# The last block's order by row halves, its stores on two queues, and one tile of batch 4 placed 1.2 slots later

## The chip, the core and the metric

The kernel runs on one core of one Trainium2 chip. The metric is the device time of that core in microseconds (us), as the median of repeated executions. One further execution was taken with the hardware profiler; all rows shown below are from that one.

The core's engines appear in the profile as PE (TensorE matmul), PEld (TensorE weight load), DVE (VectorE), ACT (ScalarE), POOL (GpSimd) and SP (SyncE, which here only issues DMAs). SPq and ACTq are the DMA issues on the queues of SP and ACT.

## What is computed

For each of 8 batches and 8 heads, with 576 positions and a head size of 64:

```python
kv  = einsum('bhsd,bhse->bhde', k, v)
out = einsum('bhsd,bhde->bhse', q, kv)
out = out / sqrt(mean(out*out, -1) + 1e-6) * g_norm      # -> x, 512 columns per position
xn  = (x - mean(x)) / sqrt(var(x) + 1e-6) * g_ln
y   = x + relu(xn @ w_ch1) @ w_ch2                       # 512 -> 2048 -> 512
```

## The kernel before

**Blocks.** The 8 x 576 rows are worked on as nine blocks of 512 rows, four tiles of 128 rows each: one block for the first 512 rows of each batch, and a last block, "rem", that gathers the 64 remaining rows of all eight batches. A block has two stages on PE: `mm1` (line 684; 512 to 2048, ReLU on ACT) and the second product (2048 to 512). The tiles of block b+1 are prepared while block b is on PE: matmul `o_ps` (line 302), square on ACT (`sq`, line 308), sum on DVE (`ss`, line 379), root on ACT (`rms`, line 387), then on DVE the reciprocal (`inv`, line 394), two scalings (lines 383 and 401), the negated mean (line 405) and the centred copy `xc` (line 426), and a DMA transpose from SP (line 437) that gives `xT_blk`. The variance (`dev`, line 419) is an ACT instruction of its own.

**The second product in seven products.** From block 1 on, the second product is a two-by-two block product made of seven half-sized products instead of eight. Its row sums S1, S2, S4, S3 are DVE additions (lines 515 to 518, `row_sums`), made in three pieces; the last piece is placed at the first four ticks of the second stage. Blocks 1 to 7 go through `mm2_seven` (line 547). Block 3 uses the order p1, p4, p6, p5, p2, p3, p7. Of these, p6 multiplies S2 into `p_y`, DVE then reads `p_y` into `u2` (line 566), and p3 adds S3's product to the same bank, so p3 cannot start before that reading.

**The order of work.** Instructions are emitted in program order to each engine, and each engine takes its own in that order. PE's loops call `tick()` (line 778), and an agenda written out by hand puts everything else at a slot, which `at` (line 769) turns into a tick: a block has 16 ticks for `mm1` and, from block 1 on, 14 for the seven products, so slots past 16 of a block shrink by 14/16. Within a tick the agenda's entries are sorted by slot, and the row sums have -1, which puts them first. `plan_tile` (line 455) places a tile's first part (`o_ps`, `sq`, `ss`) at a slot, its second part (root to `xc`) two slots later, its transpose at 4.5 slots later, and its variance at a slot of its own. `keep_q` (line 234), a POOL copy of the batch's remaining q rows, is placed half a slot after the last tile's first part.

The lines that place batch 4's tiles are 965 to 972. They are reached while block 3 is on PE.

**The last block.** `mm2_seven_last` (line 621) takes the two tiles of each half one after the other instead of together. For tile t it does p_x, p_q, p_y, p_z and the second part of p_y, after which DVE writes the two halves of a lower-row tile (`o(1, 0)`, `o(1, 1)`, line 651), which `put(1)` stores; then the second part of p_x and p_l, after which DVE writes an upper-row tile, which `put(0)` stores. Tile 0 is finished wholly before tile 1 starts. `store` (line 731) makes two DMAs of 64 partitions for the last block, one always on SP, the other on the queue given as `upper`. Tile 1's last product and its last store are cut in two column halves.

Of the kernel before, what the change touches and what calls it, by code (L numbers as in the profile page):

```python
# [14 lines left out]
def kernel(  # L15
# [11 lines left out]
    nc = tc.nc  # L27
    f32 = mybir.dt.float32
    bf16 = mybir.dt.bfloat16
    AF = mybir.ActivationFunctionType  # L30
    ALU = mybir.AluOpType
# [26 lines left out]
    ps_m = ctx.enter_context(tc.psum_pool(name="ps_m", bufs=1))  # L58
    ps_out = ctx.enter_context(tc.psum_pool(name="ps_out", bufs=2))
    ps1 = ctx.enter_context(tc.psum_pool(name="ps1", bufs=3))  # L60
    ps2 = ctx.enter_context(tc.psum_pool(name="ps2", bufs=2))
# [172 lines left out]
    def keep_q(b):  # L234

        nc.gpsimd.tensor_copy(qj[:, b], qts.pop(b)[:, J, :, :64])
# [203 lines left out]
    def main_tile(b, j, pool=None, tag="ops"):  # L440
        q_t, kvp = qts[b], held[b]
        if b not in blks:
            blks[b] = new_block()
        return Tile([(slice(0, 128), lambda hp: q_t[:, j, hp, :], kvp)], blks[b], j, pool, tag)
# [41 lines left out]
    H2, C2 = nDe // 2, Dm // 2  # L486
# [5 lines left out]
    def m1_q(b, rows, odd):  # L492
        return m1s[b][:, odd::2, rows * 256:rows * 256 + 256]

    def w2_q(odd, cols):
        return w2_sb[:, odd::2, cols * C2:cols * C2 + C2]
# [24 lines left out]
    def product(dst, a, w, start, stop, ts=(0, 1), c0=0, c1=256):  # L521


        for t in ts:
            tick()
            for i in range(H2):
                nc.tensor.matmul(dst[:, t - ts[0], :c1 - c0], lhsT=a[:, i, t * 128:(t + 1) * 128],  # L527
                                 rhs=w[:, i, c0:c1], start=start and t == ts[0] and i == 0,
                                 stop=stop and t == ts[-1] and i == H2 - 1,
                                 skip_group_check=True)  # L530

    def outs(b):
        x_blk = blks[b][0]
        o_sb = [outp.tile([128, 2, Dm], f32, tag="osb", name="o_sb") for _ in range(2)]

        def x(rows, cols):
            return x_blk[:, 2 * rows:2 * rows + 2, cols * C2:cols * C2 + C2]

        def o(rows, cols):
            return o_sb[rows][:, :, cols * C2:cols * C2 + C2]  # L540

        return x, o, o_sb

    def half(pool, tag, name):
        return pool.tile([128, 2, C2], f32, tag=tag, name=name)
# [75 lines left out]
    def mm2_seven_last(b):  # L621
        V, G = nc.vector, nc.gpsimd
        S1, S2, S3, S4 = sums.pop(b)
        a11, a12, a22 = m1_q(b, 0, 0), m1_q(b, 0, 1), m1_q(b, 1, 1)
        b11, b21, b22 = w2_q(0, 0), w2_q(1, 0), w2_q(1, 1)
        x_all, _, o_sb = outs(b)
        v0_t, v1_t, qv_t, w22_t, u2_t = (half(fpool, n, n) for n in ("v0", "v1", "u3", "r5", "u2"))
        banks = (((ps1, "p1"), (ps1, "p1"), (ps2, "p2"), (ps2, "p2"), (ps_m, "misc")),
                 ((ps1, "p1"), (ps1, "p1"), (ps_out, "ops"), (ps_out, "ops"), (ps1, "p1"),
                  (ps2, "p2")))  # L630
        for t in range(2):
            def x(rows, cols):
                return x_all(rows, cols)[:, t]

            def o(rows, cols):
                return o_sb[rows][:, t, cols * C2:cols * C2 + C2]

            def part(dst, a, w, start, stop, c0=0, c1=C2):
                product(dst, a, w, start, stop, (t,), c0, c1)

            def put(rows, c0=0, c1=Dm, upper=nc.scalar):
                store(b, 2 * rows + t, o_sb[rows][:, t:t + 1], c0, c1, upper)

            ends = ((0, C2),) if t == 0 else ((0, C2 // 2), (C2 // 2, C2))
            p_x, p_q, p_y, p_z, *p_l = (pool.tile([128, 1, C2], f32, tag=tag, name="p_s")
                                        for pool, tag in banks[t])
            v0, v1, qv, w22, u2 = (a[:, t] for a in (v0_t, v1_t, qv_t, w22_t, u2_t))
            r0, r1 = (rstds[b][:, 2 * rows + t:2 * rows + t + 1] for rows in range(2))

            def scaled_add(dst, src, r, other):  # L650
                V.scalar_tensor_tensor(dst, in0=src, scalar=r, in1=other,
                                       op0=ALU.mult, op1=ALU.add)

            part(p_x, a11, b11, True, False)
            nc.scalar.activation(v1, p_x[:, 0], func=AF.Copy, scale=r1)
            nc.scalar.activation(v0, p_x[:, 0], func=AF.Copy, scale=r0)
            G.tensor_add(w22, v1, x(1, 1))
            part(p_q, a22, T4, True, True)
            scaled_add(qv, p_q[:, 0], r1, v1)
            G.tensor_add(qv, qv, x(1, 0))  # L660
            part(p_y, S2, T2, True, False)
            scaled_add(u2, p_y[:, 0], r0, v0)
            G.tensor_add(u2, u2, x(0, 1))
            part(p_z, S1, T1, True, True)
            scaled_add(w22, p_z[:, 0], r1, w22)
            scaled_add(u2, p_z[:, 0], r0, u2)
            part(p_y, S3, T3, False, True)
            scaled_add(o(1, 0), p_y[:, 0], r1, qv)
            scaled_add(o(1, 1), p_y[:, 0], r1, w22)
            put(1)  # L670
            part(p_x, a12, b21, False, True)
            scaled_add(o(0, 0), p_x[:, 0], r0, x(0, 0))
            if t:
                put(0, 0, C2)
            for p, (c0, c1) in zip(p_l, ends):
                part(p, S4, b22, True, True, c0, c1)
                scaled_add(o(0, 1)[:, c0:c1], p[:, 0, :c1 - c0], r0, u2[:, c0:c1])
            if t:
                put(0, C2)
            else:  # L680
                put(0, upper=nc.sync)
            del p, p_l, p_x, p_q, p_y, p_z

    def mm1(b, t0, n, c0=0, c1=nDe):
        blk, m1 = blks[b], m1_of(b)
# [45 lines left out]
    def store(b, ts, o_sb, c0=0, c1=Dm, upper=None):  # L731

        n = o_sb.shape[1]
        if b == "rem":
            dst = out[:, :S_LO, :].rearrange("(t f) (p j) e -> f j p t e", j=JJ, f=2)[:, J]
            for half, engine in enumerate((nc.sync, upper)):
                engine.dma_start(dst[half, :, ts:ts + n, c0:c1],
                                 o_sb[half * 64:half * 64 + 64, :, c0:c1])
            return
        eng = nc.gpsimd if b == 0 or b == 1 and ts >= 2 else nc.sync  # L740
        for half in range(2):
            src = o_sb[half * 64:half * 64 + 64, :, c0:c1]
            if b == 0:
                j = 2 * ts + half
                dst = (out[b, :S_LO, :].rearrange("(p j) e -> p j e", j=JJ)[:, j:j + 1] if ts < 2
                       else out[b, S_LO:, :].rearrange("(p j) e -> p j e", j=J)[:, j - J:j - J + 1])
            else:
                dst = (out[b, S_LO:, :].rearrange("(p j) e -> p j e", j=J) if half else
                       out[b, :S_LO, :].rearrange("(p j) e -> p j e", j=JJ))[:, ts:ts + n]
            eng.dma_start(dst[:, :, c0:c1], src)  # L750
# [18 lines left out]
    def at(slot, fn):  # L769

        i, r = divmod(slot, 32)
        blocks = [*range(B), "rem"]
        if r > 16 and i < len(blocks) and blocks[int(i)] in SEVEN:
            r = 16 + (r - 16) * 14 / 16
        s = sum(30 if x in SEVEN else 32 for x in blocks[:int(i)]) + r
        agenda.setdefault(int(s + 1e-6), []).append((s, fn))

    def tick():
        for _, fn in sorted(agenda.pop(clock[0], []), key=lambda e: e[0]):
# [17 lines left out]
    t = [main_tile(0, 0)] + [main_tile(0, i, *((ps1, "p1"), (ps_m, "misc"), (ps2, "p2"))[i - 1])  # L797
                             for i in range(1, 4)]
# [163 lines left out]
    at(268, lambda: rstd_of("rem"))  # L962


    for b, at_q, at_o in ((3, 52, (68.5, 72.5, 76.5, 83)), (4, 81, (96.5, 102.7, 109, 115)),
                          *((b, 32 * b - (46.4 if b == 5 else 47.2), tuple(32 * b - i for i in (34.5, 27.3, 20.1, 12.9)))
                            for b in range(5, B))):
        at(at_q, lambda b=b: turn_q_dma(b))
        for j, o in enumerate(at_o):
            plan_tile(o, lambda b=b, j=j: main_tile(b, j), o + 4.5, False, 32 * b - 13.4 + 3.5 * j)  # L970
        at(at_o[-1] + .5, lambda b=b: keep_q(b))
        at(32 * b + 6, lambda b=b: rstd_of(b))
# [15 lines left out]
    for ts in range(4):  # L988
        p2 = p2s[ts]
# [46 lines left out]
```

## Time and profile before

| | |
|---|---|
| median of 3 runs (lowest to highest) | 278.20 us (278.18 to 278.21) |
| the profiled execution's own time | 278.19 us |
| its span in the trace | 276.0 us |
| PE busy | 268.8 us (97%) |
| DVE, ACT, POOL busy | 197.7, 185.5, 116.6 us |
| block 3's stretch on PE, 107.39 to 135.92 us | 28.53 us |
| the last block's seven products start at | 259.53 us |

The profile's span is the time in the trace from the core's first to its last instruction; the execution's time is 2.2 us longer. In the rows, "start us, us" are an instruction's start from the span's start and its length; a merged row covers several instructions of one kind (x8). "[0.18 <-DVE u L566]" says that the engine was idle for 0.18 us just before, and what released it. Instructions of one engine are pipelined, so that the next may start before the last has ended. Matmul ends are modelled.

### The profile page before, as it was taken

Reading aid. Unit: us, or ns where it says so; the run is one execution under the profiler, and the core shown is the slowest. Engines: PE = TensorE matmul, PEld = TensorE weight load, DVE = VectorE, ACT = ScalarE, POOL = GpSimd, SP = SyncE. Lnnn points to the kernel's source line nnn. Section 1 sums busy time; section 2 is a strip of 40 time slices with the busy share of each in tenths; the row PEclk is TensorE's granted clock in tenths of the full one; section 3 lists DMA queues with packets and bytes.
Section 4 is the critical chain, followed back from the end, with each engine's and each line's share of the span. In section 5 each row is a group of like instructions: output and inputs, shape, how many; then the busy total and the mean of one; then the engine's idle time right before and its main releaser. Section 6 shows DMA issues by size and latency. Waiting matters only on the chain.

```text
span 276.0 us, 6784 instructions
## 1 busy us (share of the span) xinstructions
PE 268.8 (97%) x2674; PEld 194.8 (71%) x2674; DVE 197.7 (72%) x464; ACT 185.5 (67%) x414; POOL 116.6 (42%) x143
## 2 busy tenths in 40 slices
PE   8899999999999999999999999999999999999993
PEld 3589855999889986468745874587458745874683
DVE  6676437897996895999679856985797379823564
ACT  3567755898759685768576857786877487746610
POOL 8842440991099007901870196017101800280140
PEclk9999999999999999999999999999999999999999
DMA  7999999979979993996299829960711161005032
GB/s 215 199 207 205 197 194 192 202 179 194 113 123 158 184 187 83 151 221 125 31 190 252 116 34 189 246 118 19 171 21 20 21 171 21 20 19 154 1 76 78
DMA packets 63880, 36.57 MB, mean 132 GB/s; under 512 B 34016, under 2 KB 60900, under 8 KB 63848
## 3 DMA queue, kind: packets, MB, share of 16 engines
q0 software_dynamic: 29104, 19.34, 47.9%
q1 hardware_dynamic: 34152, 15.81, 27.8%
q10 hardware_dynamic: 592, 0.98, 1.0%
q8 instruction: 21, 0.34, 0.5%
q14 instruction: 11, 0.09, 0.1%
HBM read 36.71 MB, written 9.44 MB: 167 GB/s over the span
## 4 chain that ended last, share of the span: by engine, by line
PE 84%; DVE 7%; DMA 4%; ACT 2%; issue 1%; POOL 1%; DVEq 0%; POOLq 0%
PE p L694 41%; PE p_y L527 8%; PE p_z L527 8%; PE p_x L527 8%; PE p L716 5%; PE p_s L527 4%; DMA w_sb<-in_moe_w_ch_dram 4%; PE p_q L527 4%; PE o_ps L302 2%; PE kv_ps L275 2%; DVE ss L379 1%; DVE S L517 1%; ACT m L697 1%; DVE o_ps L383 1%; DVE x_blk L401 1%
## 5 line engine op out<-in xcount | busy, mean ns | idle before, releaser
L694 PE MATMUL p<-xT_blk,w_sb 128*128 128x128 bf16 (+2 forms) x1024 | 131.7, 286 | 0.6 <-DMA w_sb<-in_moe_w_ch_dram 0.3
L694 PEld LDWEIGHTS <-w_sb 128*128 128x128 bf16 x1024 | 78.7, 98 | 44.9 <-issue 0.7
L697 ACT ACTIVATE m<-p 128x512 bf16<-128x512 f32 x144 | 85.5, 598 | 35.2 <-PE p L694 33.0
L527 PEld LDWEIGHTS <-m 128*128 128x128 bf16 x512 | 49.4, 98 | 7.7 <-issue 0.6
L379 DVE TENSOR_REDUCE ss<-sq 128x8 f32<-128x512 f32 x35 | 23.8, 680 | 24.6 <-ACT sq L308 24.4
L527 PEld LDWEIGHTS <-S 128*128 128x128 bf16 x392 | 37.5, 98 | 4.5 <-DVE S L516 0.3
L582 POOL TENSOR_TENSOR q<-q,x_blk 128x512 f32<-128x512 f32 x5 | 6.4, 1290 | 69.7 <-ACT q L561 69.7
L527 PE MATMUL p_x<-w_sb,m 128*128 128x256 bf16 x224 | 27.3, 273 | 0.0
L419 ACT ACTIVATE dev<-x_blk,st_blk 128x512 f32<-128x512 f32 x36 | 26.0, 722 | 0.3 <-DVE st_blk L405 0.2
L609 POOL TENSOR_TENSOR u<-u,x_blk 128x512 f32<-128x512 f32 x7 | 8.9, 1268 | 39.5 <-DVE u L566 39.5
L383 DVE TENSOR_TENSOR o_ps<-o_ps,inv 128x512 f32<-128x512 f32 x33 | 23.1, 700 | 3.1
L401 DVE SCALAR_TENSOR_TENSOR x_blk<-o_ps,g_norm_sb 128x512 f32<-128x512 f32 x33 | 22.8, 691 | 1.1
L308 ACT ACTIVATE sq<-o_ps 128x512 f32<-128x512 f32 x35 | 21.0, 599 | 3.6 <-PE o_ps L302 3.6
L515 DVE TENSOR_TENSOR S<-m 128x768 bf16<-128x768 bf16 (+2 forms) x22 | 12.7, 582 | 12.2 <-ACT m L697 12.2
L426 DVE TENSOR_SCALAR xc<-x_blk,st_blk 128x512 bf16<-128x512 f32 x32 | 18.6, 581 | 1.1
L387 ACT ACTIVATE rms<-ss,eps_sb 128x8 f32<-128x8 f32 x36 | 10.8, 299 | 11.7 <-DVE ss L379 11.3
L566 DVE SCALAR_TENSOR_TENSOR u<-p_y,rstd,v 128x256 f32<-128x256 f32 x28 | 12.2, 476 | 5.3 <-PE p_y L527 5.3
L716 PE MATMUL p<-w_sb,m 128*128 128x512 bf16 x64 | 15.0, 379 | 0.0
L561 ACT ACTIVATE v<-p_x,rstd 128x256 f32<-128x256 f32 x28 | 11.0, 478 | 5.3 <-PE p_x L527 5.3
L527 PE MATMUL p_y<-T,m 128*128 128x256 bf16 x112 | 13.9, 272 | 0.2 <-DVE u L566 0.2
L527 PE MATMUL p_z<-w_sb,S 128*128 128x256 bf16 x112 | 13.5, 273 | 0.0
L527 PE MATMUL p_y<-T,S 128*128 128x256 bf16 x112 | 13.5, 273 | 0.0
(149 smaller groups left out, 367.6 us busy)
## 6 DMA issues: line engine op xcount, KB each, us to landing
out_dram<-o_sb SPq DMA_DIRECT2D x26, 256.0 KB, 4.5
w_sb<-in_moe_w_ch_dram POOLq DMA_DIRECT2D x6, 512.0 KB, 13.7
q_in<-in_q_dram POOLq DMA_DIRECT2D x7, 320.0 KB, 6.5
k_in<-in_k_dram POOLq DMA_DIRECT2D x7, 320.0 KB, 7.7
v_in<-in_v_dram POOLq DMA_DIRECT2D x7, 320.0 KB, 9.9
q_in<-in_q_dram POOLq DMA_DIRECT2D x8, 256.0 KB, 7.2
k_in<-in_k_dram POOLq DMA_DIRECT2D x7, 256.0 KB, 8.4
v_in<-in_v_dram POOLq DMA_DIRECT2D x7, 256.0 KB, 12.3
```

The costliest lines, as they stand in the source:

```text
L308: nc.scalar.activation(self.sq_t, self.o_ps, func=AF.Square)
L379: nc.vector.tensor_reduce(self.ss, self.sq_t, axis=AX.X, op=ALU.add)
L383: nc.vector.tensor_mul(self.o_ps, self.o_ps, self.inv().to_broadcast([128, H, D]))
L401: nc.vector.scalar_tensor_tensor(x_blk[:, ts].rearrange("p (h d) -> p h d", h=H), in0=self.o_ps, scalar=1.0, in1=g_norm_sb.to_broadcast([1 ...
L419: nc.scalar.activation(dev, x_blk[:, ts], func=AF.Square, bias=st[:, 1, ts:ts + 1], accum_out=st[:, 2, ts:ts + 1])
L426: nc.vector.tensor_scalar_add(self.xc_t, x_blk[:, self.ts], st[:, 1, self.ts:self.ts + 1])
L515: for i, fn in enumerate((lambda: nc.vector.tensor_add(S1, a21, a22), lambda: nc.vector.tensor_sub(S2, S1, a11), lambda: nc.vector.tensor_ ...
L527: nc.tensor.matmul(dst[:, t - ts[0], :c1 - c0], lhsT=a[:, i, t * 128:(t + 1) * 128], rhs=w[:, i, c0:c1], start=start and t == ts[0] and i ...
L566: V.scalar_tensor_tensor(dst[:, t], in0=src[:, t], scalar=rstd[:, 2 * rows + t:2 * rows + t + 1], in1=other[:, t], op0=ALU.mult, op1=ALU.add)
L694: nc.tensor.matmul(p1[:, i, :], lhsT=w1_sb[:, kk, de * 128:(de + 1) * 128], rhs=blk[2][:, kk, sl], start=(kk == 0), stop=(kk == nK - 1))
L697: nc.scalar.activation(m1[:, de0:de0 + per, sl], p1, func=AF.Relu)
L716: nc.tensor.matmul(p2[:, c0:c1], lhsT=m1s[b][:, de, ts * 128:(ts + 1) * 128], rhs=w2_sb[:, de, c0:c1], start=(de == 0), stop=(de == nDe - 1))
```

## The change

Two things change.

First, `mm2_seven_last`: its loop body becomes a generator with two stages, run in the order tile 0, tile 1, tile 0, tile 1. So both tiles' lower rows come first and both tiles' upper rows after them. The PSUM banks of p_q, p_y and p_z are given back after the first stage, and p_l's are taken in the second, from `ps_m` for tile 0 and from `ps1` and `ps2` for tile 1. The second DMA of the stores of tile 0 changes its queue: for the lower rows from ACT to SP, for the upper rows from SP to ACT. Products, additions and DMAs are the same in number and size.

Second, the first part of batch 4's last tile moves from slot 115 to 116.2. With it move its second part (117 to 118.2), its transpose (119.5 to 120.7) and `keep_q(4)` (115.5 to 116.7).

```diff
--- before.py
+++ after.py
@@ -625,32 +625,34 @@
         b11, b21, b22 = w2_q(0, 0), w2_q(1, 0), w2_q(1, 1)
         x_all, _, o_sb = outs(b)
         v0_t, v1_t, qv_t, w22_t, u2_t = (half(fpool, n, n) for n in ("v0", "v1", "u3", "r5", "u2"))
-        banks = (((ps1, "p1"), (ps1, "p1"), (ps2, "p2"), (ps2, "p2"), (ps_m, "misc")),
-                 ((ps1, "p1"), (ps1, "p1"), (ps_out, "ops"), (ps_out, "ops"), (ps1, "p1"),
-                  (ps2, "p2")))
-        for t in range(2):
+        banks = (((ps1, "p1"), (ps1, "p1"), (ps2, "p2"), (ps2, "p2")),
+                 ((ps1, "p1"), (ps_out, "ops"), (ps_out, "ops"), (ps2, "p2")))
+        ends = (((ps_m, "misc", 0, C2),),
+                ((ps1, "p1", 0, C2 // 2), (ps2, "p2", C2 // 2, C2)))
+
+        def scaled_add(dst, src, r, other):
+            V.scalar_tensor_tensor(dst, in0=src, scalar=r, in1=other, op0=ALU.mult, op1=ALU.add)
+
+        def tile_of(t):
+
             def x(rows, cols):
                 return x_all(rows, cols)[:, t]
 
             def o(rows, cols):
                 return o_sb[rows][:, t, cols * C2:cols * C2 + C2]
 
+            def bank(pool, tag):
+                return pool.tile([128, 1, C2], f32, tag=tag, name="p_s")
+
             def part(dst, a, w, start, stop, c0=0, c1=C2):
                 product(dst, a, w, start, stop, (t,), c0, c1)
 
             def put(rows, c0=0, c1=Dm, upper=nc.scalar):
                 store(b, 2 * rows + t, o_sb[rows][:, t:t + 1], c0, c1, upper)
 
-            ends = ((0, C2),) if t == 0 else ((0, C2 // 2), (C2 // 2, C2))
-            p_x, p_q, p_y, p_z, *p_l = (pool.tile([128, 1, C2], f32, tag=tag, name="p_s")
-                                        for pool, tag in banks[t])
+            p_x, p_q, p_y, p_z = (bank(*e) for e in banks[t])
             v0, v1, qv, w22, u2 = (a[:, t] for a in (v0_t, v1_t, qv_t, w22_t, u2_t))
             r0, r1 = (rstds[b][:, 2 * rows + t:2 * rows + t + 1] for rows in range(2))
-
-            def scaled_add(dst, src, r, other):
-                V.scalar_tensor_tensor(dst, in0=src, scalar=r, in1=other,
-                                       op0=ALU.mult, op1=ALU.add)
-
             part(p_x, a11, b11, True, False)
             nc.scalar.activation(v1, p_x[:, 0], func=AF.Copy, scale=r1)
             nc.scalar.activation(v0, p_x[:, 0], func=AF.Copy, scale=r0)
@@ -667,19 +669,28 @@
             part(p_y, S3, T3, False, True)
             scaled_add(o(1, 0), p_y[:, 0], r1, qv)
             scaled_add(o(1, 1), p_y[:, 0], r1, w22)
-            put(1)
+            put(1, upper=nc.scalar if t else nc.sync)
+            del p_q, p_y, p_z
+            yield
             part(p_x, a12, b21, False, True)
             scaled_add(o(0, 0), p_x[:, 0], r0, x(0, 0))
             if t:
                 put(0, 0, C2)
-            for p, (c0, c1) in zip(p_l, ends):
+            for pool, tag, c0, c1 in ends[t]:
+                p = bank(pool, tag)
                 part(p, S4, b22, True, True, c0, c1)
                 scaled_add(o(0, 1)[:, c0:c1], p[:, 0, :c1 - c0], r0, u2[:, c0:c1])
+                del p
+            del p_x
             if t:
                 put(0, C2)
             else:
-                put(0, upper=nc.sync)
-            del p, p_l, p_x, p_q, p_y, p_z
+                put(0)
+            yield
+
+        tiles = [tile_of(0), tile_of(1)]
+        for t in (0, 1, 0, 1):
+            next(tiles[t])
 
     def mm1(b, t0, n, c0=0, c1=nDe):
         blk, m1 = blks[b], m1_of(b)
@@ -962,7 +973,7 @@
     at(268, lambda: rstd_of("rem"))
 
 
-    for b, at_q, at_o in ((3, 52, (68.5, 72.5, 76.5, 83)), (4, 81, (96.5, 102.7, 109, 115)),
+    for b, at_q, at_o in ((3, 52, (68.5, 72.5, 76.5, 83)), (4, 81, (96.5, 102.7, 109, 116.2)),
                           *((b, 32 * b - (46.4 if b == 5 else 47.2), tuple(32 * b - i for i in (34.5, 27.3, 20.1, 12.9)))
                             for b in range(5, B))):
         at(at_q, lambda b=b: turn_q_dma(b))
```

## Prediction

> **What bounds the kernel now.** I read the page's busy times first, then the stretches of the blocks, then the chain of work that ended last, and at last the order of time at the two places that the change touches.
>
> ```profile
> PE 268.8 (97%) x2674; PEld 194.8 (71%) x2674; DVE 197.7 (72%) x464; ACT 185.5 (67%) x414; POOL 116.6 (42%) x143
> ```
>
> PE is busy for 97% of the span, so a change that leaves PE's work alone can gain in three kinds of places only: before PE has data, where PE waits inside, and after its last matmul. The change touches one place of the second kind and the one of the third. The busy time by stretch (us; then each engine's busy time and its instructions; the number after POOL is PE's granted clock, then the DMA share and GB/s) shows the inner one:
>
> ```profile
> 107.39:135.92 28.53, 28.35 (x238) 18.81 (x235) 23.83 (x51) 20.93 (x47) 15.60 (x19) 1.00 0.85 141
> 135.92:163.71 27.79, 27.79 (x233) 18.75 (x232) 21.12 (x49) 20.09 (x45) 13.12 (x16) 1.00 0.88 145
> ```
>
> The clock is full in both. Block 3 (the first) takes 28.53 us, block 4 27.79, with PE busy throughout. It is also the one with the most DVE work, and the chain runs over DVE there:
>
> ```profile
> 127.85 0.99 DVE m L518
> ...
> 131.20 0.80 DVE u L566 x2
> 132.04 1.03 PE p_y L527 x8
> ```
>
> PE starts p3 (p_y, L527) when DVE has read `p_y` into u2 (L566), and u2 stands on DVE behind the whole second part of batch 4's last tile. That is the tile that moves. The same place in order of time:
>
> ```profile
> 117.15 0.72 POOL L236 COPY qj<-qt 128x256 bf16<-128x256 bf16 x1
> 123.46 0.39 PE L302 MATMUL o_ps<-kv_pack,qt 128*128 128x128 bf16 x4
> 125.81 0.61 ACT L308 ACTIVATE sq<-o_ps 128x512 f32<-128x512 f32 x1
> 126.28 0.86 ACT L561 ACTIVATE q<-p_q,rstd 128x256 f32<-128x256 f32 x2
> 126.84 0.42 DVE L517 TENSOR_TENSOR S<-m,S 128x512 bf16<-128x512 bf16 x1
> 127.17 0.68 DVE L379 TENSOR_REDUCE ss<-sq 128x8 f32<-128x512 f32 x1
> 127.29 1.27 POOL L582 TENSOR_TENSOR q<-q,x_blk 128x512 f32<-128x512 f32 x1 [9.43 <-ACT q L561]
> 127.77 1.07 DVE L518 TENSOR_TENSOR m<-m 128x512 bf16<-128x512 bf16 x1
> 127.89 0.30 ACT L387 ACTIVATE rms<-ss,eps_sb 128x8 f32<-128x8 f32 x1 [0.74 <-DVE ss L379]
> 128.09 0.71 ACT L419 ACTIVATE dev<-x_blk,st_blk 128x512 f32<-128x512 f32 x1
> 128.71 0.19 ACT L419 ACTIVATION_READ_ACCUMULATOR dev<-x_blk,st_blk 128x1 f32 x1
> 128.77 0.19 DVE L394 RECIPROCAL inv<-rms 128x8 f32<-128x8 f32 x1
> 130.81 1.05 PE L527 MATMUL p_x<-w_sb,m 128*128 128x256 bf16 x8
> 131.12 0.87 DVE L566 SCALAR_TENSOR_TENSOR u<-p_y,rstd,v 128x256 f32<-128x256 f32 x2
> 132.04 1.03 PE L527 MATMUL p_y<-T,m 128*128 128x256 bf16 x8 [0.18 <-DVE u L566]
> ```
>
> Look at S3 (L518): 1.07 us, while S4 (L517), the same size, took 0.42. S3 started at 127.77, half a microsecond into POOL's addition (L582, to 128.56), and ended 0.28 us after it: it stood behind POOL for about 0.65 us. Eight matmuls of this form follow each other every 0.87 us (269.85 to 270.72 in the last block's rows, below), so p3 could have started at 130.81 + 0.87 = 131.68; it started at 132.04. The loss is 0.36 us; the row shows only 0.18 as idle because the end of a matmul is modelled.
>
> The other place is the end:
>
> ```profile
> 269.85 1.04 PE L527 MATMUL p_s<-w_sb,m 128*128 128x256 bf16 x8
> 270.72 1.06 PE L527 MATMUL p_s<-w_sb,S 128*128 128x128 bf16 x16
> 270.92 0.48 DVE L651 SCALAR_TENSOR_TENSOR o_sb<-p_s,rstd,x_blk 128x256 f32<-128x256 f32 x1
> 271.37 0.80 DVE L651 SCALAR_TENSOR_TENSOR o_sb<-p_s,rstd,u 128x128 f32<-128x128 f32 x2
> ```
> ```profile
> 270.99 0.47 SPq L737 DMA_DIRECT2D out_dram<-o_sb  x1
> 270.99 0.50 ACTq L737 DMA_DIRECT2D out_dram<-o_sb  x1
> ...
> 271.58 0.79 ACTq L737 DMA_DIRECT2D out_dram<-o_sb  x1
> ...
> 272.19 0.54 SPq L737 DMA_DIRECT2D out_dram<-o_sb  x1
> 272.47 0.56 ACTq L737 DMA_DIRECT2D out_dram<-o_sb  x1
> ```
> ```profile
> out_dram<-o_sb ACTq DMA_DIRECT2D x1, 64.0 KB, 2.8
> ...
> out_dram<-o_sb ACTq DMA_DIRECT2D x1, 64.0 KB, 2.3
> ```
> ```profile
> 272.20:274.40 2.20, 0.00 (x0) 0.00 (x0) 0.00 (x0) 0.00 (x0) 0.00 (x0) 1.00 0.80 229
> ```
>
> The last matmul ends at 270.72 + 1.06 = 271.78, DVE's last write at 271.37 + 0.80 = 272.17. SP issues its half of the last store at once (272.19), ACT 0.28 us later (272.47), because its issue before (271.58, 0.79 long) was still running. The two rows of landing times are those of ACT's issues at 271.58 and 272.47. The last lands at about 272.47 + 2.3 = 274.8; the other 1.2 us are closing work. From 272.20 to 274.40 no engine works and the DMA engines are busy for 80%: six stores leave within 1.5 us of each other, and queue. That one 64 KB store takes 2.8 us and the other 2.3 shows it.
>
> **The change part by part.** *Batch 4's tile.* In ticks, the first part goes from 110 to 111, the second from 112 to 113, the transpose from 114 to 115, `keep_q` from 111 to 112. No instruction is added. What changes places on each queue: on PE, `o_ps` stands 8 matmuls (0.87 us) later, at about 124.33 to 124.72; `sq` on ACT started only at 125.81, so that costs nothing, and if ACT were free it would cost DVE nothing before 127.5. On SP the transpose keeps its neighbours. On DVE, S3 (tick 111, first in its tick) now stands ahead of `ss`; u2 stays behind the second part, because it is emitted after both ticks of p6. On ACT, the variance of tile 1 (L419, slot 113.34 in ticks) now stands ahead of the root (113.43). On POOL, `keep_q`'s copy now stands behind the addition L582, not ahead of it.
>
> DVE, step by step: S3 starts where `ss` did, 127.17 (0.33 after S4). POOL's addition starts 0.12 us later, at 127.29, so S3 should be through before POOL gets in its way: 0.42, as S4. The rows for that order are those of the next block, S3 ahead of the same addition by 0.23 us:
>
> ```profile
> 155.36 0.41 DVE L518 TENSOR_TENSOR m<-m 128x512 bf16<-128x512 bf16 x1
> ...
> 155.59 1.31 POOL L582 TENSOR_TENSOR q<-q,x_blk 128x512 f32<-128x512 f32 x1 [12.45 <-ACT q L561]
> ```
>
> There S3 kept its 0.41 and POOL took 0.04 more. So `ss` starts at 127.17 + 0.33 = 127.50 and ends at 128.18; the root starts 0.04 later, as in its row (127.85 to 127.89), and ends at 128.52; `inv` starts at 128.56 instead of 128.77. DVE now waits for ACT there, which gives back two thirds of the 0.65 us that S3 saves. ACT's variance ahead of the root (0.71 + 0.19 from 127.14) is through at about 128.04, before `ss` ends. The rest of the chain is unchanged, so u2 and p3 come 0.21 us sooner, and 0.15 of the 0.36 us stay. `keep_q`'s copy (0.72 at most) runs at about 128.7 to 129.4; DVE's work then reads PSUM, and `xc` comes only after 130. Block 4 has PE busy throughout, and I find no idle time of PE behind it, so PE carries 0.21 us to the end. Bounds: 0 (something else holds `inv`) to 0.36 (the whole wait). I take **0.21**.
>
> *The last block.* PE does the same matmuls in another order, with the last three pieces the same; DVE's last writes follow PE as before, since one tile's upper row gives DVE 0.96 us of work in 1.75 us of PE. The banks that come back were read more than 1 us earlier. So DVE's last write stays at 272.17 (less the 0.21), and nothing is won before it. What changes is the traffic ahead of the last store. Tile 1's lower-row store goes out 1.75 us earlier (269.24), and in its place stands tile 0's upper-row store: its last product ends one tile's upper row before the end, so DVE is done at about 270.57, and the pair leaves at 270.59 instead of 270.99. Tile 1's first column half leaves when DVE has written it (270.92 + 0.48 = 271.40), 0.15 us sooner on ACT, onto queues that are free; ACT's issue, 0.50 to 0.55 long there, is then over before 272.17, and the last one goes at 272.19 on both: 0.28 us sooner. If the landing time stays 2.3, that is the gain. From below: both halves now leave at the same time, and the row of an ACT issue that left 0.04 us or so beside one of SP's is the 2.8; with 2.8 the last landing would be 274.99, 0.22 later than now. From above: if the stretch is a queue that drains at its own rate, everything in it moves by as much as its head, 0.40. The 2.8 belongs to a store with three others issued in the 0.6 us ahead of it, and the head start of 0.40 thins that; the DMA share of 80% is near a queue that drains at its own rate. I take **0.38**, near the upper end. Moving the second lower-row DMA to SP costs SP one more issue of 0.5 us at 265.5, with nothing due on it until 269.2; it spares ACT an issue ahead of tile 1's scalings, which is why those do not wait.
>
> The sum against the profiled execution: 278.19 - 0.21 - 0.38 = **277.6 us**; the median of the runs shown, 278.20, is the same.
>
> **The rivals.** (a) *POOL gets in first.* S3's lead over POOL's addition is 0.12 us. If the addition begins first, S3 waits for its end and is over where it was before, 128.84; only then `ss` (0.09 before S3's end, as behind S4, to 129.43), root to 129.77, `inv` at 129.81, which is 1.04 us later than before, and all of it lands on p3. With the tail's gain: 278.19 + 1.04 - 0.38 = 278.85. For it: 0.12 us is little. Against it: POOL starts on ACT's `q`, whose time does not depend on the moved tile, and DVE's S4 sets S3's.
>
> The Trainium skill (SBUF — State Buffer, section "SBUF: two separate sides") says that a DVE instruction with two SBUF inputs and a GpSimd instruction that reads SBUF hold a shared port pair by an exclusive lock, for the whole instruction, and that the one that starts first gets it. The trace agrees: S3 took 1.07 us behind the addition and 0.41 ahead of it. By that rule this rival turns on the order of the two starts alone, and no run yet shows it with 0.12 us between them.
>
> (b) *The tile's move brings nothing:* the root still holds `inv` at its old time because ACT is later than I count. Only the tail: 278.19 - 0.38 = 277.8. (c) *The end does not do what it says:* the last two halves, issued together, get in each other's way and land no sooner than now. Only the tile: 278.19 - 0.21 = 278.0. (d) *More than forecast:* the whole wait of 0.36 goes and the tail gains its 0.40 in full: 277.4.
>
> **How the numbers follow.** Forecast 0.60, (a) 0.14, (b) 0.10, (c) 0.08, (d) 0.08. About 0.2%, or 0.56 us, is what a measurement of this kernel can tell from no change, so the line for faster is 277.64, and the forecast's 0.59 us stand just beyond it: I count 0.40 of its 0.60 as faster and 0.20 as no difference. Faster: 0.40 + 0.08 = 0.48. Same: 0.20 + 0.10 + 0.08 = 0.38. Slower: (a), 0.14. The range goes from 277.4 (both upper bounds, 0.76) to 278.2 (the tile's 0.21 against the tail's lower bound of -0.22); it leaves out (a).
>
> **What would show it.** In the changed profile: S3 (L518) near 127.2 with 0.42 us ahead of POOL's addition; `inv` near 128.56; p3 about 0.2 us sooner and block 3's stretch near 28.3 us; the pair of stores near 270.4, the last issues on SP and ACT together, some 0.02 after DVE's last write; a last landing of 2.1 to 2.2 us. S3 still over 1 us, p3 later than 132.04, or a last issue on ACT 0.3 us behind SP's would prove the steps wrong.

## The result and the profile after

The changed kernel takes 277.79 us (median of 22 runs, 277.56 to 278.54), the kernel before 278.38 us in the runs beside it (22 runs, 278.15 to 279.27). The ratio is 0.9978, with a 95% interval of 0.9972 to 0.9984: 0.22% or 0.61 us faster, between 0.45 and 0.78. The forecast was 0.59 us. The profiled execution took 277.76 us, its span is 275.6 us.

The changed kernel's order of time at block 3's second stage answers to the fifteen lines shown of before. In this execution the whole of block 3 runs 0.09 us later than in the one before, a difference that is there before the second block starts. So compare distances from the start of the stage's first product, p_x, which before stood here:

```profile
121.71 1.91 PE L527 MATMUL p_x<-w_sb,m 128*128 128x256 bf16 x16
```

The changed kernel ("..." stands for rows left out):

```profile
121.80 1.91 PE L527 MATMUL p_x<-w_sb,m 128*128 128x256 bf16 x16
...
127.26 0.42 DVE L518 TENSOR_TENSOR m<-m 128x512 bf16<-128x512 bf16 x1
127.37 1.43 POOL L582 TENSOR_TENSOR q<-q,x_blk 128x512 f32<-128x512 f32 x1 [10.10 <-ACT q L561]
...
127.59 0.68 DVE L379 TENSOR_REDUCE ss<-sq 128x8 f32<-128x512 f32 x1
...
128.30 0.30 ACT L387 ACTIVATE rms<-ss,eps_sb 128x8 f32<-128x8 f32 x1 [0.37 <-DVE ss L379]
128.63 0.20 DVE L394 RECIPROCAL inv<-rms 128x8 f32<-128x8 f32 x1 [0.37 <-ACT rms L387]
...
131.93 1.03 PE L527 MATMUL p_y<-T,m 128*128 128x256 bf16 x8
```

S3 (L518) now stands ahead of `ss`, starts 0.11 us ahead of POOL's addition and takes 0.42 us instead of 1.07; POOL's addition pays 0.16 us for it (1.43). DVE, which did not wait for the root before, now waits 0.37 us for it. p3 (the last row) starts 10.13 us after p_x, 10.33 before: 0.20 us gained.

The changed kernel's stretches of block 3 and block 4 (us, then busy time and instructions by engine):

```profile
107.48:135.81 28.33, 28.23 (x235) 18.79 (x235) 23.14 (x51) 20.85 (x47) 15.42 (x19) 1.00 0.84 142
135.81:163.60 27.79, 27.68 (x231) 18.76 (x232) 21.13 (x49) 20.08 (x45) 13.14 (x16) 1.00 0.95 145
```

Block 3 went from 28.53 to 28.33 us, block 4 is unchanged. (A few matmul records are missing from this trace, so PE's busy time reads low.) The changed kernel's end: DVE's last writes, the issues on the two queues, and the landing times of the two 64 KB stores on ACT:

```profile
271.31 0.80 DVE L634 SCALAR_TENSOR_TENSOR o_sb<-p_s,rstd,u 128x128 f32<-128x128 f32 x2
```
```profile
270.50 0.47 SPq L748 DMA_DIRECT2D out_dram<-o_sb  x1
270.51 0.50 ACTq L748 DMA_DIRECT2D out_dram<-o_sb  x1
...
271.38 0.51 ACTq L748 DMA_DIRECT2D out_dram<-o_sb  x1
...
272.14 0.47 SPq L748 DMA_DIRECT2D out_dram<-o_sb  x1
272.14 0.62 ACTq L748 DMA_DIRECT2D out_dram<-o_sb  x1
```
```profile
out_dram<-o_sb ACTq DMA_DIRECT2D x1, 64.0 KB, 2.5
...
out_dram<-o_sb ACTq DMA_DIRECT2D x1, 64.0 KB, 2.2
```

DVE's last write ends at 271.31 + 0.80 = 272.11, and now both queues issue 0.03 us later; ACT was 0.30 us late before. The last landing comes at about 272.14 + 2.2 = 274.3. From DVE's last write to the last landing it is 2.24 us by the trace's landings, 2.58 before: 0.34 us gained.

### The profile page after: what moved, and what is told of

Its sections match the earlier page's. It is cut to its first block, busy times and chain, and to the rows that moved or that the text cites. A ratio compares the mean times of both kernels' runs of the same rounds, so it can differ in the third digit from the quotient of the medians.

```text
span 275.6 us, 6767 instructions
## 1 busy us (share of the span) xinstructions
PE 268.7 (97%) x2658; PEld 195.1 (71%) x2674; DVE 196.8 (71%) x464; ACT 185.4 (67%) x414; POOL 115.9 (42%) x143
## 4 chain that ended last, share of the span: by engine, by line
PE 93%; DMA 2%; DVE 2%; ACT 2%; issue 1%; SPq 0%; DVEq 0%
PE p L705 44%; PE p_x L527 9%; PE p_y L527 9%; PE p_z L527 9%; PE p L727 5%; PE p_s L527 4%; PE p_q L527 4%; PE o_ps L302 3%; PE kv_ps L275 2%; DMA gn_row<-in_g_norm_dram 2%; ACT m L708 1%; PE tp L204 0%; PE p L218 0%; PE tp L433 0%; ACT xT_blk L435 0%
```

## The experiments

Two kinds of theory were put against each other. Mine: the change is two separate gains, one of 0.2 us because S3 gets ahead of POOL's addition, one of 0.35 us because the last stores are issued sooner and find a thinner queue. The rivals: the whole gain belongs to one part; the exchange of queues carries the end; at block 3 the moved `o_ps` or `keep_q` counts, not S3. Ratios are to the kernel before, with 95% intervals; runs of one comparison shared their runs of the kernel before.

### The two parts alone

The tile's move alone, and the last block alone:

```diff
 e1_tile_only: the kernel before, with
-(96.5, 102.7, 109, 115)
+(96.5, 102.7, 109, 116.2)
```
```diff
 e2_last_block_only: the changed kernel, with
-(96.5, 102.7, 109, 116.2)
+(96.5, 102.7, 109, 115)
```

> The kernel before with batch 4's last tile at slot 116.2 and nothing else. Theory (the two parts add up: S3 gets ahead of POOL's addition): S3 near 127.2 us with 0.42 us, p3 0.20 us sooner than in the kernel before, the end unchanged; 0.2 us faster, ratio 0.9993. Rival (the whole gain is the last block's, and what p3 wins is lost again at a later wait of PE): 0.0 us, ratio 1.000.

> The change without the tile's move (batch 4's last tile at slot 115). Theory: from DVE's last write to the end of the span 0.34 us less than the 3.88 us of the kernel before, S3 still 1.07 us; 0.35 us faster, ratio 0.9987. Rival (the parts need each other: with p3 unchanged, the end is all there is, and it is worth all of the change): 0.55 us faster, ratio 0.998.

Measured: e1 0.9990 (0.9982 to 0.9999), e2 0.9987 (0.9978 to 0.9995). Their product, 0.9977, is the change's 0.9978. Each interval is wider than the effect itself, so the traces have to say which part does what. In e1's trace p3 starts 10.15 us after p_x (131.84 after 121.69) and the end is that of before (2.56 us from DVE's last write to the last landing). In e2's S3 takes 1.06 us, p3 is as late as before (10.33 us after p_x), and the last landing comes 2.28 us after DVE's last write. Each part does its share without the other, so they are separate and add up.

### Which part of the tile's move

The kernel before with S3 ahead of `ss` and nothing else moved, and the changed kernel with S3 put back behind it:

```diff
 e5_s3_first_only: the kernel before; e6_s3_behind_ss: the changed kernel
-row_sums(b, SPLIT[i - 1] // 2, SPLIT[i] // 2, range(4))
+row_sums(b, SPLIT[i - 1] // 2, SPLIT[i] // 2, (0, 1, 2, 2) if b == 3 and i == 3 else range(4))   # e5
+row_sums(b, SPLIT[i - 1] // 2, SPLIT[i] // 2, (0, 1, 2, 4) if b == 3 and i == 3 else range(4))   # e6
```

> The kernel before with one exchange on DVE alone: in block 3 the last piece of S3 is placed one tick sooner and so stands ahead of the sum ss of batch 4's last tile; the tile, its variance, its root and keep_q keep their places. Theory (only the order of S3 and ss against POOL's addition counts): S3 0.42 us, POOL's addition some 0.13 us longer, p3 0.20 us sooner; ratio 0.9993. Rival (the later o_ps, or keep_q's copy leaving its place ahead of the addition, carries it): S3 and p3 as before, ratio 1.000.

> The changed kernel with S3's last piece in block 3 one tick later, so that it stands behind ss again; everything else of the change is kept. Theory: S3 about 1.07 us again behind POOL's addition, inv about 128.8, p3 as late as in the kernel before; what is left is the end's 0.35 us, ratio 0.9987. Rival (the tile's place counts, not S3's): p3 stays 0.2 us sooner, ratio 0.998.

Measured: e5 0.9989 (0.9980 to 0.9997), as much as the whole move of the tile; e6 0.9984 (0.9975 to 0.9993), which by itself does not tell the theory's 0.9987 from the rival's 0.998. The traces do. e5, where the tile, its root and `keep_q` keep their places:

```profile
121.73 1.91 PE L527 MATMUL p_x<-w_sb,m 128*128 128x256 bf16 x16
...
127.18 0.42 DVE L518 TENSOR_TENSOR m<-m 128x512 bf16<-128x512 bf16 x1
127.31 1.41 POOL L582 TENSOR_TENSOR q<-q,x_blk 128x512 f32<-128x512 f32 x1 [9.43 <-ACT q L561]
...
131.85 1.03 PE L527 MATMUL p_y<-T,m 128*128 128x256 bf16 x8
```

and e6, where everything has moved but S3:

```profile
121.86 1.91 PE L527 MATMUL p_x<-w_sb,m 128*128 128x256 bf16 x16
...
127.44 1.27 POOL L582 TENSOR_TENSOR q<-q,x_blk 128x512 f32<-128x512 f32 x1 [10.10 <-ACT q L561]
127.91 1.08 DVE L518 TENSOR_TENSOR m<-m 128x512 bf16<-128x512 bf16 x1
...
132.19 1.03 PE L527 MATMUL p_y<-T,m 128*128 128x256 bf16 x8 [0.18 <-DVE u L566]
```

From p_x to p3 it is 10.12 us in e5 and 10.33 us in e6, 10.13 in the changed kernel and 10.33 before. S3's place ahead of POOL's addition is the whole of this part; the 1.2 slots are only the way in which it got there.

### Order or queues

The new order with the old queues, and the old order with the new ones:

```diff
 e3_order_old_queues: the last block as changed (tile at 115), with
-            put(1, upper=nc.scalar if t else nc.sync)
+            put(1)
-                put(0)
+                put(0, upper=nc.sync)
```
```diff
 e4_queues_old_order: the kernel before, with
-            put(1)
+            put(1, upper=nc.scalar if t else nc.sync)
-                put(0, upper=nc.sync)
+                put(0)
```

> The last block in the new order, with the old queues (tile 0's lower rows on SP and ACT, its upper rows on SP twice), and the tile at slot 115. Theory (the order thins the queue at the end; the queues of tile 0's stores matter little): ACT's last issue still together with SP's, SP's first column half some 0.15 us late behind the second issue, end 0.25 to 0.35 us sooner than before, ratio 0.9990. Rival (the exchange of queues carries the gain): no more than 0.05 us, ratio 0.9998 or above.

> The kernel before in its old order, with the new queues for tile 0's stores alone (lower rows on SP twice, upper rows on SP and ACT). Theory: tile 0's stores have landed before 270 us in the old order, so nothing at the end changes; an issue of 0.5 us on ACT near 266.2 delays tile 1's first scaling by 0.2 us at most, which PE does not wait for; 0.0 us, ratio 1.000. Rival (the exchange of queues carries the gain): 0.3 us faster, ratio 0.9989.

Measured: e3 0.9988 (0.9979 to 0.9997), e4 0.9998 (0.9989 to 1.0007). In the old order the exchange of queues gives nothing. In the new order the times cannot tell the old queues (e3) from the new ones (e2, 0.9987), but the traces can: with the old queues the late issue returns, on the other queue. e3's last issues, and ACT's landing time:

```profile
271.08 0.59 SPq L748 DMA_DIRECT2D out_dram<-o_sb  x1
...
271.76 0.56 SPq L748 DMA_DIRECT2D out_dram<-o_sb  x1
...
272.20 0.47 ACTq L748 DMA_DIRECT2D out_dram<-o_sb  x1
272.42 0.55 SPq L748 DMA_DIRECT2D out_dram<-o_sb  x1
```
```profile
out_dram<-o_sb ACTq DMA_DIRECT2D x1, 64.0 KB, 2.0
```

DVE's last write ended at 272.17 there. SP has four issues in a row, each held by the one before, and its last is 0.25 us late; from DVE's last write to the last landing it is 2.44 us, between the 2.24 of the change and the 2.58 of before. From DVE's last write to the end of the span it is 3.88 us before, 3.67 in e3 and 3.57 in e2. So of the 0.31 us that e2 gains there, the order alone brings 0.21; the other 0.10 come from the queues, which bring it only in the new order. This miss of mine (I had SP's first half late and the last on time) already says that the issue of the last store counts.

### Does the queue count?

The changed kernel without one of the stores ahead:

```diff
 e7_one_store_less: the changed kernel, with
-            else:
-                put(0)
             yield
```

> The changed kernel without the store of tile 0's upper rows: these 128 rows of the output are left unwritten. It empties the queue ahead of the last two stores. Theory (the stores drain as a queue, and the change thinned it without emptying it): the last landing comes 0.15 to 0.3 us sooner than the changed kernel's 2.2 us after its issue. Rival (only ACT's issue on time counted; landing after an issue is fixed): landing 2.2 us after the issue as before, the same time as the changed kernel.

Measured: 0.9968 (0.9956 to 0.9980). The last issues and their landings:

```profile
272.14 0.47 SPq L746 DMA_DIRECT2D out_dram<-o_sb  x1
272.15 0.64 ACTq L746 DMA_DIRECT2D out_dram<-o_sb  x1
```
```profile
out_dram<-o_sb SPq DMA_DIRECT2D x1, 64.0 KB, 2.0
out_dram<-o_sb ACTq DMA_DIRECT2D x1, 64.0 KB, 2.2
```

ACT's last store lands 2.2 us after its issue, as with 256 KB more ahead of it; from DVE's last write it is 2.24 us in both. My theory of the queue falls for the last store: taking one away ahead of it does not move its landing. The stores between do feel it: tile 1's first column half lands 1.95 us (SP) and 2.23 us (ACT) after its issue in e7, 2.33 and 2.49 in the changed kernel. The rival holds: the last landing comes about 2.2 us after the last issue, and what the change wins is above all that this issue is 0.27 us less late. That agrees with the Trainium skill (DMA: Bandwidth & Descriptors, section "Issuing engines are not separate DMA queues"), which says that several issuing engines save only the time of the issue itself, as all of them share the same DMA engines.

Yet the ratio lies 0.1% below the change's 0.9978, which neither theory expected; the two intervals touch, so the times alone do not show it. The trace has the place, after the landing: from the last landing to the end of the span it is 1.30 us before and after, and 1.11 us here. SP closes there with one wait after another for the DMAs' completion counts, some 0.06 us each and always in the same order. There are eight counts, given out in turn, so that two DMAs less give the last two stores other ones. Before and after, the last store on ACT has the count that stands second in the row: it lands last, and six waits still follow. In e7 it has the eighth, with no wait behind it; but now SP's last store has the first, and as that one lands only 0.24 us ahead of ACT's, the row of waits behind it is what holds the end.

### The closing waits

So four DMAs more, far from the end, should move the last stores' counts again:

```diff
 e11_four_more_issues: the changed kernel, in store
+            if b == 7:
+                for i in range(n):
+                    eng.dma_start(dst[:, i:i + 1, c0:c1], src[:, i:i + 1])
+                continue
             eng.dma_start(dst[:, :, c0:c1], src)
```

> The changed kernel with batch 7's four stores cut in two each, near 248 us, on SP, which is idle there: four DMAs more, nothing else. The eight completion counts of the DMAs are given out in turn, so that the last two stores get two others, and SP's closing waits, some 0.06 us each in a fixed order, then have their last landing nearer their end. Theory (the end after the last landing is this row of waits): from the last landing to the end 0.25 us less, landing itself as in the changed kernel; ratio to the kernel before 0.9969. Rival (the end after the last landing is fixed): ratio 0.9978.

Measured: 0.9965 (0.9953 to 0.9977). e11's end:

```profile
271.11 0.80 DVE L634 SCALAR_TENSOR_TENSOR o_sb<-p_s,rstd,u 128x128 f32<-128x128 f32 x2
...
271.94 0.62 ACTq L748 DMA_DIRECT2D out_dram<-o_sb  x1
```
```profile
out_dram<-o_sb ACTq DMA_DIRECT2D x1, 64.0 KB, 2.2
```

The landing again takes 2.2 us (to about 274.17 by the trace), and the span ends at 275.2: 1.04 us after it instead of 1.30. ACT's last store now has the sixth count of the row, so two waits follow its landing and not six: four times 0.06 us, the expected 0.25 us. e3 agrees: there SP's store lands last, with the third count and five waits behind it, and the end takes 1.23 us. By the times the gain over the change is less sure, because e11's interval and the change's (0.9972 to 0.9984) overlap.

### What is left at block 3

The change leaves about 0.16 us of p3's wait, and as much at p6, whose S2 DVE finishes late. In the changed kernel's rows sixteen matmuls of this form follow each other in 1.75 us and eight in 0.87, but from the start of p6 (p_y, T and S) to the next product it is 1.92 us, and from the second half of p_x to p3 1.03 us:

```profile
125.51 2.08 PE L527 MATMUL p_y<-T,S 128*128 128x256 bf16 x16
...
127.43 1.91 PE L527 MATMUL p_z<-T,S 128*128 128x256 bf16 x16
...
130.90 1.05 PE L527 MATMUL p_x<-w_sb,m 128*128 128x256 bf16 x8
131.00 0.87 DVE L566 SCALAR_TENSOR_TENSOR u<-p_y,rstd,v 128x256 f32<-128x256 f32 x2
...
131.93 1.03 PE L527 MATMUL p_y<-T,m 128*128 128x256 bf16 x8
```

Three kernels went for that:

```diff
 e8_u2_first: the changed kernel, batch 4's last tile's second part at slot 119.2 (behind p6)
-            plan_tile(o, lambda b=b, j=j: main_tile(b, j), o + 4.5, False, 32 * b - 13.4 + 3.5 * j)
+            late = b == 4 and j == 3
+            plan_tile(o, lambda b=b, j=j: main_tile(b, j), o + 4.5, False, 32 * b - 13.4 + 3.5 * j,
+                      119.2 if late else None)
 e9_p7_ahead_of_p3, e10_p5_and_p7_sooner: the changed kernel, in block 3
-(p1, p4, p6, p5, p2, p3, p7)
+(p1, p4, p6, p5, p2, p7, p3)   # e9
+(p1, p4, p5, p6, p2, p7, p3)   # e10
```

> The changed kernel with the second part of batch 4's last tile placed behind p6, so that DVE reads p_y into u2 ahead of the root's successors. Theory (DVE's queue holds p3): u2 comes near 128.3 us, p3 starts with no wait, another 0.15 us sooner; the transpose of the tile leaves about 0.9 us later, near 132.0, and lands by 134.6, ahead of block 4; against the kernel before 0.7 us, ratio 0.9975. Rival (the wait moves on: block 4's first matmul then waits for the late transpose, or the last block's for its own): as the changed kernel, ratio 0.998, or worse.

> The changed kernel with p7 ahead of p3 in block 3, so that 1.75 us of PE's work stand between p_x and the product that waits for u2; DVE's order is otherwise kept. Theory (u2 is the only thing that p3 still waits for): the 0.16 us that are left of p3's wait go; block 4 starts 0.16 us sooner than in the changed kernel; ratio to the kernel before 0.9972. Rival (as in the kernel with u2 first, the wait moves on to the tile's transpose): block 4 starts no sooner, ratio 0.9978.

> The changed kernel with the order p1, p4, p5, p6, p2, p7, p3 in block 3: also p5 ahead of p6, so that S1 is used first and S2 has 1.75 us more. Theory (block 3 loses 0.16 us at S2 and 0.16 us at p3, and both waits are DVE's order alone): both go, block 4 starts 0.32 us sooner than in the changed kernel and block 3 takes as long as block 4 but for one o_ps; ratio to the kernel before 0.9966. Rival (the transpose of batch 4's last tile, which lands 2.0 us ahead of its use, or the one of the last block, which PE waited for by 0.06 us, takes the gain back): ratio 0.9975 or above.

Measured: e8 1.0001 (0.9992 to 1.0010), e9 0.9972 (0.9962 to 0.9981), e10 0.9964 (0.9951 to 0.9978). In e8 p3 does start with no wait, 9.97 us after p_x, but the rival held:

```profile
131.31 1.27 POOL L582 TENSOR_TENSOR r<-r,x_blk 128x512 f32<-128x512 f32 x1
...
131.75 1.12 DVE L426 TENSOR_SCALAR xc<-x_blk,st_blk 128x512 bf16<-128x512 f32 x1
...
132.89 1.19 SPq L437 DMA_TRANSPOSE xT_blk<-xc  x1
...
136.90 1.89 PE L705 MATMUL p<-xT_blk,w_sb 128*128 128x512 bf16 x8 [0.35 <-PE p_z L527]
```

With u2 early, POOL's next addition is early too and now meets `xc`, which takes 1.12 us instead of 0.49 and ends 0.28 us after the addition, as S3 did before the change. The transpose leaves late, and block 4's first matmul waits for it: from p_x to that matmul it is 14.20 us, against 13.84 in the changed kernel. Fifteen of the transpose's sixteen completions came by 135.32, the last at 136.81, 1.5 us after them, and one of the DMA engines was fetching 16 KB of instructions from 134.73 for 1.05 us. The other traces show this transpose without a late piece, and in each of them the fetch begins only after its first completion. That the fetch held the last piece is read from these times, not tested.

e9 and e10 keep DVE's order and move PE's instead. Their intervals overlap the change's, so again the traces have to tell. From p_x to block 4's first matmul it is 14.04 us before, 13.84 in the changed kernel, 13.70 in e9 and 13.53 in e10. e10's rows:

```profile
121.73 1.91 PE L527 MATMUL p_x<-w_sb,m 128*128 128x256 bf16 x16
...
135.26 2.10 PE L705 MATMUL p<-xT_blk,w_sb 128*128 128x512 bf16 x8
```

In e10 both waits are gone, as expected. The last kernel joins e10 and e11:

> The changed kernel with both: block 3's order p1, p4, p5, p6, p2, p7, p3 and batch 7's stores cut in two. Theory (the gains lie apart and add up): 0.6 + 0.32 + 0.25 us, ratio to the kernel before 0.9958. Rival (a wait of PE between takes the first back): 0.997.

Measured: 0.9961 (0.9949 to 0.9973), not to be told from e10 or e11 alone, nor from the sum expected (0.9958), nor from the rival's 0.997. In its profiled execution, the longest of its six, both gains are there (13.53 us at block 3, 1.05 us after the last landing), but 0.2 us were lost between, where the last block begins. e12's rows there, the changed kernel's, and those of the kernel before:

```profile
216.55 1.91 PE L527 MATMUL p_z<-w_sb,S 128*128 128x256 bf16 x16
218.49 1.02 PE L705 MATMUL p<-xT_blk,w_sb 128*128 128x512 bf16 x3
```
```profile
216.31 1.91 PE L527 MATMUL p_z<-w_sb,S 128*128 128x256 bf16 x16
218.11 1.02 PE L705 MATMUL p<-xT_blk,w_sb 128*128 128x512 bf16 x3
```
```profile
216.42 1.91 PE L527 MATMUL p_z<-w_sb,S 128*128 128x256 bf16 x16
218.17 1.03 PE L694 MATMUL p<-xT_blk,w_sb 128*128 128x512 bf16 x4
```

Sixteen matmuls of p_z take 1.75 us in PE's rhythm; it is 1.94 us here and 1.80 in the changed kernel. PE waits there for the last completion of a transpose, and starts 0.135 us after it in both. An instruction fetch is on one DMA engine again (from 215.7, 1.17 us long, in the changed kernel). The kernel before had its last completion at 217.94 and the first matmul at 218.17, with no wait, and 0.1 us of room. Whether this wait comes differs from one execution to the next: over the fourteen traces the last completion comes 3.91 to 4.37 us after the transpose's issue, and PE waits, by 0.02 to 0.20 us, in the four in which it is 4.19 us or more. e1, e5 and e10, which reach this place as early or earlier, lost nothing there.

All three of e10, e11 and e12 are faster than the kernel before. Their intervals overlap that of the change, so their gain over it rests on the traces; which of them is fastest stays open.

## Why the prediction was right, and where it was not

**S3 and block 3.** Right in each step: S3 ahead of POOL's addition with 0.42 us, the wait for the root that gives most of it back, `inv` 6.83 us after p_x (forecast 6.85), 0.20 us at p3 (forecast 0.21). e5 and e6 show that S3's place alone does it. POOL's addition paid 0.16 us where I took 0.04 from the next block's rows, and p3 came as forecast all the same. Rival (a), that POOL gets in first, did not come: in all six profiled executions with S3 in the new place on the old product order, its lead of 0.09 to 0.13 us was enough. Rival (b), that the tile's move brings nothing, falls with e1, and (d), that the whole 0.36 us go, with the 0.16 us left at p3.

**"PE carries 0.21 us to the end."** It does, but not in every execution: in the profiled one 0.06 us were lost at the last block's first matmul, in those of e1 and e5 nothing. I had looked for idle time of PE and found none; a transpose that lands 0.1 us ahead of its use leaves no idle time and yet has hardly any room.

**The end.** The order of events was right: the pair of stores at 270.5, the last issues together 0.03 us after DVE's write, landing 2.2 us later. The term was 0.38 and measured 0.34, and the reason given for choosing it near the upper end was wrong: "a queue that drains at its own rate". The two rows of 2.8 and 2.3 us, and a DMA share of 80%, made me see a queue; e7 shows that the last landing does not move when a store ahead of it is left out. What the sum held in its first half, ACT's issue 0.28 us sooner, measured 0.27. The landing itself got 0.07 us shorter (2.28 to 2.21 after its issue) where I had counted on 0.10; whether thinner traffic is the cause of that no run shows. Rival (c), that the two halves issued together land no sooner, did not come.

**The sum.** 0.21 + 0.38 = 0.59 us stood against 0.61 us (0.45 to 0.78). The parts as the traces have them, 0.20 + 0.34, less the 0.06 lost in that execution, come to 0.48 to 0.54 us, which is inside the interval too. So the terms are right to within a few hundredths, and that the sum meets the median within 0.02 us is partly luck. The spans of the two profiled executions are only 0.39 us apart, as the changed one was also 0.09 us late before its second block. The median of 277.79 lies above the forecast 277.6 because the kernel before was 278.38 in the runs beside it and not 278.20.

## What to carry to other kernels

When an engine that sets the pace loses time beside another engine, look which instruction of the two comes first and by how much: exchanging two neighbours in one engine's queue (e5) was worth as much here as moving a whole tile (e1). At the end of a kernel, count the issues on each queue back from the last store: here the last store left 0.3 us late and cost about that, while 256 KB less in flight ahead of it did not move its landing. Before you free a wait, look for the next deadline behind it: one that is met just in time shows as no wait at all, as the last block's transpose did, which landed 0.1 us ahead of need.

## What the runs showed of the hardware that was not expected

- The end after the last landing is not fixed. It takes 1.30 us when the store that lands last has the second of the eight counts in SP's row of closing waits, 1.23 with the third (e3) and 1.04 with the sixth (e11). In e7 it takes 1.11 us, held by the store with the first count, which lands 0.24 us ahead of the last.
- Instruction fetches (16 KB each, 0.9 to 1.9 us on one DMA engine in the changed kernel's trace, 21 in a run) seem to hold one sixteenth of a transpose. In all fourteen traces the last block's transpose has a fetch that begins before its first completion, and its last completion comes 1.5 to 2.0 us behind the fifteenth; block 4's transpose has both in e8 alone. Other transposes met a fetch and were not held, and no run moved a fetch, so this is not shown. PE felt it in e8 and, at the last block, in four traces.
- In the last block an issue on SP takes 0.47 us when no other stands right before it and 0.54 to 0.60 right behind another; on ACT it is 0.47 to 0.64 and 0.55 to 0.79 us. So three or four in a row set the time of the last.
